# The weight conversions begin four steps earlier in a fused attention and expert kernel

## The chip, the core and the metric

The kernel runs on one core of a Trainium2 chip. The metric is the device time in microseconds, the median of three runs. The engines are named TensorE (PE in the rows, PEld its weight loads), VectorE (DVE), ScalarE (ACT), GpSimd (POOL) and SyncE (SP, whose queue issues all loads and stores here).

## The reference

Three layers follow one another: causal attention for 2 batches, 12 heads, 448 positions and 64 elements a head; a soft mixture of 8 experts with 4 slots each; and a gated product with three weight matrices, whose float64 elements the kernel reads as pairs of 32-bit words.

```python
scores = q @ k.T / sqrt(64); scores = where(causal, scores, -1e9)
attn = exp(scores - max); attn /= attn.sum + 1e-9; x = attn @ v        # x: 896 x 768
logits = x @ phi
d = softmax of logits over the tokens;  slot_input = d.T @ x           # 8 experts x 4 slots
for e in range(8): slot_out[e] = relu(slot_input[e] @ w1[e]) @ w2[e]
c = softmax of logits over the slots;   x = c @ slot_out
out = ((x @ w_a) * (x @ w_b)) @ w_out                                   # weights are float64
```

## The kernel before

**Pairs and steps.** Attention runs over 12 pairs of heads (`it` 0 to 11), each in four steps (`g` 0 to 3); a 13th round, `it` 12, only finishes the last pair. All instructions are written out by hand in the order in which each engine runs them. In a step of pair `it` TensorE makes score blocks (line 249, tile `s`), VectorE their negated maxima (lines 255 and 259, `nm`), ScalarE the exponentials with their sums (line 269, `p`), VectorE the reciprocals (lines 279 and 280, `rc`), and GpSimd scales the tiles by them (line 283). In the four steps of the next pair, TensorE transposes these tiles (line 296, `t`) and ScalarE copies them out (line 299, `pT`). In step 0 of the pair after that, TensorE multiplies them with the values (line 328, `v`), and ScalarE copies the product (line 332, `xT`). The product of pair 10 has fill matmuls before and within it (line 307), whose results nothing reads.

**Conversions.** A float64 weight matrix is read as tiles of 768 KB, `raw` 0 to 35, each half of a matrix block. A conversion is made of two activations on ScalarE (lines 162 and 163; in round 12 two GpSimd instructions, lines 155 and 158, in their place) and of two instructions on VectorE (lines 193 and 196). The VectorE part of a tile is written one conversion later than its ScalarE part, but when no tile below 32 is left to begin, what is still open is finished at once:

```python
while len(fin) > (lag if conv and conv[0] < limit else 0):
```

At the end of every step one conversion is begun, if the step's number is above `CVOFF` and the table `CVN` says so (three steps of four):

```python
step += 1
if step > CVOFF:
    conv_step(CVN[step % len(CVN)], LAG, NT1, "pool" if (it, g) > LASTQ else "act")
```

**Loads.** All loads are issued by SyncE, in the order of a list: `raw` tiles go round the four slots `r0` to `r3`, with a few expert weights (`w`) between them; a slot is loaded again when what it held has been used. After the 32 `raw` tiles, the four slots take expert weights. The next expert weights go to the slots `q0` to `q3` and then to `t0` and `t1`. These lie where the attention stage had its tiles, so that their loads wait for the end of that stage. The experts' matmuls (line 632, `h`, and line 673, `so`) use a tile, and its slot is loaded again.

Of the kernel before, what the change touches and what calls it, by code (L numbers as in the profile page):

```python
# [41 lines left out]
    (("rect", 28, 4, 0, 28), ("tri", 6, 2), ("sq", 28, 4)),  # L42
    (("sq", 8, 16),),
)
CVOFF = 7
NWARM = 32
NW2 = 4
LAG = 1
# [40 lines left out]
def moe_kernel(ctx: ExitStack, tc: tile.TileContext, pk, vt, phi, w1, w2, wab, wo, rsel, out):  # L89
# [94 lines left out]
    def conv_step(n, lag=LAG, limit=36, low="act"):  # L184
        for _ in range(n):
            if conv and conv[0] < limit:
                i = conv.pop(0)
                dst = conv_dst(i)
                done.append(i)
                fin.append((i,) + widen(raw[i], dst, 0, 768, low))  # L190
            while len(fin) > (lag if conv and conv[0] < limit else 0):
                i, di, b, ph = fin.pop(0)
                nc.vector.scalar_tensor_tensor(  # L193
                    out=b, in0=ph, scalar=-0x80000000, in1=b, op0=ALU.bitwise_and, op1=ALU.bitwise_or
                )
                nc.vector.scalar_tensor_tensor(  # L196
                    out=di, in0=di, scalar=3, in1=b, op0=ALU.logical_shift_left, op1=ALU.bitwise_or
                )
                used("raw", i)
# [288 lines left out]
    with tc.manual_schedule():  # L488
# [15 lines left out]
        for it in range(13):  # L504
            if 1 <= it < 12:
                load_v(it)
            for g in range(4):
# [25 lines left out]
# [3 lines that stand above are left out]
# [744 lines left out]
```

## Time and profile before

| | |
|---|---|
| median of 3 runs | 373.93 us (373.75 to 374.7) |
| the profiled execution | 375.18 us, with a span of 373.2 us from its first to its last instruction |
| mean granted clock of TensorE | 0.981 of full speed |
| TensorE, ScalarE, VectorE, GpSimd busy | 336.1, 206.4, 228.1 and 86.4 us of the span |
| read from memory | 87.33 MB |

The busy times are sums over the whole span, in which the stages have different limits. The attention stage ends at about 140 us; the experts and the weight products follow, and the last loads land before 280 us. The rows further down are read by stage: a row of a timeline has its start in us from the span's start, its length, the engine, the line, the operation, what it writes and reads, and, in brackets, how long the engine stood idle before it and what ended that.

### The profile page before, as it was taken

The page shows a single profiled execution, that of the slowest core. Times are in us where ns is not written, and L with a number is a line of the kernel's source. Part 1 is how long each engine was busy: PE and PEld are TensorE (multiplying, and loading weights), DVE is VectorE, ACT ScalarE, POOL GpSimd, SP SyncE. Part 2 cuts the span into 40 slices and gives each one's busy share as a digit, 9 for nine tenths or more (in the row PEclk, how much of TensorE's full clock was granted, in tenths as well). Part 3 has the DMA queues.
Part 4 walks back from the last instruction along what each step waited for, and adds up shares of the span by engine and source line. Part 5 has one row for each costly group of instructions (what it writes and reads, how often), then busy time and mean ns, then how long its engine had stood idle before and what let it go on. Part 6 is the DMA issues. An engine that isn't in the chain of part 4 may idle for free.

```text
span 373.2 us, 7002 instructions
## 1 busy us (share of the span) xinstructions
PE 336.1 (90%) x2587; PEld 205.3 (55%) x2587; DVE 228.1 (61%) x669; ACT 206.4 (55%) x475; POOL 86.4 (23%) x120
## 2 busy tenths in 40 slices
PE   8898898989989998979969889999899889999996
PEld 5564444545544655433423337543565358889995
DVE  3679999899999973020015887606956659933121
ACT  2799999999999971113007444513646742423221
POOL 2436756553556560010000000000000110301110
PEclk9999999899999999999998989999999989999999
DMA  7668799899677789999999999797920000001222
GB/s 277 269 202 284 266 336 347 289 368 304 236 271 258 243 255 355 419 419 415 417 344 374 380 364 341 245 356 225 420 122 2 0 2 0 1 2 42 86 84 84
DMA packets 20225, 90.52 MB, mean 243 GB/s; under 512 B 2336, under 2 KB 5024, under 8 KB 20192
## 3 DMA queue, kind: packets, MB, share of 16 engines
q1 hardware_dynamic: 20192, 90.09, 65.5%
q8 instruction: 20, 0.33, 0.3%
q14 instruction: 13, 0.11, 0.1%
HBM read 87.33 MB, written 2.75 MB: 241 GB/s over the span
## 4 chain that ended last, share of the span: by engine, by line
PE 45%; ACT 24%; DVE 16%; DMA 10%; issue 3%; POOL 2%; ACTq 0%; POOLq 0%; DVEq 0%
PE M L872 8%; PE o L1153 7%; ACT p L269 7%; DMA w<-in_w_dram 6%; ACT raw L163 4%; PE h L632 4%; PE ab L758 4%; DMA raw<-in_wo_dram 4%; PE so L673 3%; PE s L249 3%; ACT wab L162 3%; ACT pT L299 3%; DVE pf L814 3%; DVE pt L813 2%; PE t L296 2%
## 5 line engine op out<-in xcount | busy, mean ns | idle before, releaser
L283 POOL TENSOR_SCALAR p<-p,rc 128x448 f32<-128x448 f32 (+6 forms) x84 | 70.3, 848 | 61.3 <-DVE rc L280 28.7
L249 PE MATMUL s<-qk 64*64 64x448 f32 (+6 forms) x336 | 48.5, 403 | 0.0
L1057 POOL TENSOR_TENSOR cc<-gt,cc 128x512 fp32r<-128x512 f32 (+1 forms) x6 | 7.1, 1176 | 160.9 <-ACT cc L1056 160.9
L269 ACT ACTIVATE p<-s,nm 128x448 f32<-128x448 f32 (+6 forms) x84 | 40.4, 500 | 6.7 <-DVE nm L259 6.6
L872 PE MATMUL M<-wt,P_t 128*128 128x384 f32 x168 | 35.5, 356 | 3.7 <-DVE P_t L845 1.3
L193 DVE SCALAR_TENSOR_TENSOR raw<-raw 128x768 int32<-128x768 int32 x36 | 34.7, 965 | 4.4 <-ACT raw L163 2.6
L255 DVE TENSOR_REDUCE nm<-s 128x1 f32<-128x448 f32 (+6 forms) x84 | 31.7, 412 | 8.9 <-PE s L249 8.9
L296 PE MATMUL t<-ident,p 128*128 128x128 f32 x192 | 33.6, 293 | 2.9 <-POOL p L283 2.2
L872 PEld LDWEIGHTS M<-wt,P_t 128*128 128x128 f32 x168 | 29.2, 193 | 12.7 <-ACT wt L866 4.8
L328 PE MATMUL v<-pT,v 128*64 128x448 f32 (+3 forms) x192 | 26.9, 396 | 9.9 <-ACT pT L299 9.7
L163 ACT ACTIVATE raw<-raw 128x768 int32<-128x768 uint32 x35 | 33.0, 942 | 0.0
L632 PE MATMUL h<-w,sT 128*32 128x512 f32 x192 | 30.6, 614 | 2.0 <-ACT hs L645 1.6
L299 ACT ACTIVATE pT<-t 128x512 f32<-128x512 f32 x48 | 29.5, 620 | 2.7 <-PE t L296 2.5
L866 ACT ACTIVATE wt<-wo 128x384 fp32r<-128x384 f32 x48 | 21.8, 516 | 13.9 <-PE M L872 13.5
L867 DVE TENSOR_TENSOR wt<-wo,wt 128x384 fp32r<-128x384 f32 x48 | 23.9, 553 | 9.0 <-ACT wt L866 8.9
L249 PEld LDWEIGHTS s<-qk 64*64 64x64 f32 x336 | 20.0, 136 | 17.1 <-issue 11.0
L296 PEld LDWEIGHTS t<-ident,p 128*128 128x128 f32 x192 | 20.8, 142 | 15.4 <-POOL p L283 5.1
L758 PE MATMUL ab<-wab,sT 128*32 128x384 f32 x288 | 28.7, 517 | 0.5 <-DVE sT L597 0.5
L673 PE MATMUL so<-w,hpad 128*32 128x384 f32 x256 | 24.8, 493 | 4.2 <-DMA w<-in_w_dram 3.9
L196 DVE SCALAR_TENSOR_TENSOR wab<-wab,raw 128x768 int32<-128x768 int32 x24 | 27.1, 1130 | 0.8
L328 PEld LDWEIGHTS v<-pT,v 128*64 128x64 f32 (+1 forms) x192 | 10.9, 134 | 24.6 <-ACT pT L299 16.3
L162 ACT ACTIVATE wab<-raw 128x768 f32<-128x768 f32 x24 | 23.2, 967 | 0.0
(154 smaller groups left out, 516.2 us busy)
## 6 DMA issues: line engine op xcount, KB each, us to landing
w<-in_w_dram SPq DMA_DIRECT2D x64, 768.0 KB, 9.2
raw<-in_wab_dram SPq DMA_DIRECT2D x24, 768.0 KB, 5.0
raw<-in_wo_dram SPq DMA_DIRECT2D x12, 768.0 KB, 4.5
qk<-in_pk_dram SPq DMA_DIRECT2D x12, 448.0 KB, 5.1
v<-in_pk_dram SPq DMA_DIRECT2D x12, 192.0 KB, 4.8
out_dram<-ost SPq DMA_DIRECT2D x6, 384.0 KB, 2.3
v<-in_vt_dram SPq DMA_DIRECT2D x12, 32.0 KB, 4.5
out_dram<-ost SPq DMA_DIRECT2D x2, 192.0 KB, 1.9
```

The costliest lines, as they stand in the source:

```text
L163: nc.scalar.activation(out=pr[:, :, 0], in_=lw, func=AF.Copy, scale=2.0 ** -29, bias=-0.49999)
L193: nc.vector.scalar_tensor_tensor(out=b, in0=ph, scalar=-0x80000000, in1=b, op0=ALU.bitwise_and, op1=ALU.bitwise_or)
L249: nc.tensor.matmul(sb[r, o:o + n], lhsT=qT[r, 64 * i:64 * i + 64], rhs=kT[r, 0:n], start=False, stop=True, skip_group_check=True,)
L269: nc.scalar.activation(out=d["p"][:, POFF[i]:POFF[i] + n], in_=sb[:, o:o + n], func=AF.Exp, bias=d["nm"][:, c:c + 1], scale=0.125, accum_o ...
L283: nc.gpsimd.tensor_scalar(out=p[:, POFF[i]:POFF[i] + n], in0=p[:, POFF[i]:POFF[i] + n], scalar1=rc[:, CIX[i]:CIX[i] + 1], scalar2=1.0, op0 ...
L296: nc.tensor.transpose(ps[:, j, :], d["p"][:, o:o + 128], ident)
L299: nc.scalar.activation(out=dst, in_=ps, func=AF.Copy)
L328: nc.tensor.matmul(ps[r, 128 * kt:S], lhsT=lhsT, rhs=rhs, start=(kt == 0), stop=(kt == 3), skip_group_check=True)
L632: nc.tensor.matmul(ps[32 * g:32 * g + 32, :], lhsT=sT[:, 0, c, :], rhs=wt[8 * e + i // 3][:, 512 * (i % 3):512 * (i % 3) + 512], start=(i ...
L673: nc.tensor.matmul(so[32 * g:32 * g + 32, 0:384], lhsT=t[:, c, :], rhs=wt[8 * e + 4 + i // 4][:, 384 * (i % 4):384 * (i % 4) + 384], start ...
L758: nc.tensor.matmul(abps[q][32 * g:32 * g + 32, 0:384], lhsT=sT[:, 1, c, :], rhs=w[:, c % 2, 384 * g:384 * g + 384], start=(c == 0), stop=( ...
L872: nc.tensor.matmul(mps[k][h][:, 0:384], lhsT=l[:, f, :], rhs=r, start=(n == 0 and i == 0), stop=(n == 11 and i == 2))
```

## The change

The constant `CVOFF` goes from 7 to 3. The step's number counts from 1 with step 0 of pair 0, so the first conversion is begun in step 3 of pair 0 and no longer in step 3 of pair 1, and all later ones keep their distance.

```diff
-CVOFF = 7
+CVOFF = 3
```

What that does to the order is seen in three places. On ScalarE, from the last exponential of pair 0 on (`p0`; `raw0` is the first tile to be converted, `pT0` the copies of pair 0's transposes), before:

```order
L269 ACTIVATE p0_129,sm0_194<-s0_3_243,nm0_193 128x256
L299 ACTIVATE pT0_273<-t0_1_274 128x512
L269 ACTIVATE p1_134,sm1_225<-s1_0_263,nm1_224 128x448
L269 ACTIVATE p1_134,sm1_225<-s1_0_263,nm1_224 128x64
L299 ACTIVATE pT0_273<-t0_3_299 128x512
```

and after:

```order
L269 ACTIVATE p0_129,sm0_194<-s0_3_243,nm0_193 128x256
L162 ACTIVATE wab0_108<-raw0_182 128x768
L163 ACTIVATE raw0_182<-raw0_182 128x768
L299 ACTIVATE pT0_275<-t0_1_276 128x512
L269 ACTIVATE p1_134,sm1_225<-s1_0_265,nm1_224 128x448
L269 ACTIVATE p1_134,sm1_225<-s1_0_265,nm1_224 128x64
L162 ACTIVATE wab0_108<-raw1_188 128x768
L163 ACTIVATE raw1_188<-raw1_188 128x768
L299 ACTIVATE pT0_275<-t0_3_309 128x512
```

Tile 0 stands ahead of pair 0's first copy and tile 1 ahead of the second; in the order before, tile 0 came behind pair 1's last exponential.

On VectorE, at the end of step 0 of pair 11 and the start of its step 1 (`nm11` from `s11_1` are the maxima of step 1, those from `s11_2` of step 2), before:

```order
L193 SCALAR_TENSOR_TENSOR raw27_1412<-raw27_1412 128x768
L196 SCALAR_TENSOR_TENSOR wo1_1513<-wo1_1513,raw27_1412 128x768
L255 TENSOR_REDUCE nm11_1478<-s11_1_1586 128x1 x2
L259 TENSOR_SCALAR nm11_1478<-nm11_1478 128x2
L279 TENSOR_SCALAR rc11_1480<-sm11_1479 128x2
L280 RECIPROCAL rc11_1480<-rc11_1480 128x2
```

and after:

```order
L193 SCALAR_TENSOR_TENSOR raw30_1431<-raw30_1431 128x768
L196 SCALAR_TENSOR_TENSOR wo3_1556<-wo3_1556,raw30_1431 128x768
L193 SCALAR_TENSOR_TENSOR raw31_1474<-raw31_1474 128x768
L196 SCALAR_TENSOR_TENSOR wo3_1556<-wo3_1556,raw31_1474 128x768
L255 TENSOR_REDUCE nm11_1498<-s11_1_1609 128x1 x2
L259 TENSOR_SCALAR nm11_1498<-nm11_1498 128x2
```

Two tiles are finished ahead of step 1's maxima where one was, and the second of them is the tile that ScalarE converts in the same step 0.

On SyncE, at the end of the attention stage, before:

```order
L224 DMA v11_1543<-in_vt_dram 64x128
L148 DMA raw31_1584<-in_wo_dram 128x1536
L461 DMA w8_1640<-in_w1_dram 128x1536
L461 DMA w9_1664<-in_w1_dram 128x1536
L461 DMA w10_1728<-in_w1_dram 128x1536
L461 DMA w11_1732<-in_w1_dram 128x1536
L461 DMA w4_1804<-in_w2_dram 128x1536
```

and after:

```order
L148 DMA raw31_1474<-in_wo_dram 128x1536
L461 DMA w8_1537<-in_w1_dram 128x1536
L461 DMA w9_1561<-in_w1_dram 128x1536
L223 DMA v11_1563<-in_pk_dram 128x384
L224 DMA v11_1563<-in_vt_dram 64x128
L461 DMA w10_1603<-in_w1_dram 128x1536
L461 DMA w11_1607<-in_w1_dram 128x1536
L461 DMA w4_1804<-in_w2_dram 128x1536
```

The last `raw` tile and the first two expert weights of the ring slots now stand ahead of the values of pair 11; `w4`, the first for the slots `q0` to `q3`, follows the ring's four in both.

## Rows read from the trace of the kernel before

**Rows 1.** Attention windows: length, busy PE, PEld, DVE, ACT, POOL (count), clock, DMA, GB/s.

```profile
15.00:20.00 5.00, 5.00 (x49) 3.26 (x45) 3.30 (x14) 4.26 (x17) 2.02 (x5) 1.00 0.24 57
120.00:130.00 10.00, 9.33 (x91) 5.95 (x92) 9.48 (x23) 10.00 (x26) 6.26 (x7) 1.00 0.76 256
```

**Rows 2.** Timeline of ScalarE, pairs 0 to 2.

```profile
13.95 0.60 ACT L299 ACTIVATE pT<-t 128x512 f32<-128x512 f32 x1 [1.62 <-PE t L296]
15.83 0.60 ACT L299 ACTIVATE pT<-t 128x512 f32<-128x512 f32 x1 [0.37 <-PE t L296]
17.71 0.60 ACT L299 ACTIVATE pT<-t 128x512 f32<-128x512 f32 x1 [0.37 <-PE t L296]
20.07 0.93 ACT L162 ACTIVATE wab<-raw 128x768 f32<-128x768 f32 x1
20.88 0.94 ACT L163 ACTIVATE raw<-raw 128x768 int32<-128x768 uint32 x1
22.23 0.55 ACT L332 ACTIVATE xT<-v 128x448 f32<-128x448 f32 x1 [0.41 <-PE v L328]
23.37 0.63 ACT L269 ACTIVATE p<-s,nm 128x448 f32<-128x448 f32 x1
```

**Rows 3.** DMA issues, 3.8 to 4.2 us: count, size, us to landing.

```profile
raw<-in_wab_dram SPq DMA_DIRECT2D x1, 768.0 KB, 8.7
```

**Rows 4.** Timeline of GpSimd, pairs 1 and 10.

```profile
19.85 0.94 POOL L283 TENSOR_SCALAR p<-p,rc 128x320 f32<-128x320 f32 x2 [0.39 <-ACT pT L299]
119.67 2.42 POOL L283 TENSOR_SCALAR p<-p,rc 128x320 f32<-128x320 f32 x2 [0.73 <-ACT raw L163]
```

**Rows 5.** Timeline of ScalarE, pair 11.

```profile
124.77 0.93 ACT L163 ACTIVATE raw<-raw 128x768 int32<-128x768 uint32 x1
126.03 0.62 ACT L269 ACTIVATE p<-s,nm 128x384 f32<-128x384 f32 x1
127.40 0.66 ACT L299 ACTIVATE pT<-t 128x512 f32<-128x512 f32 x1
```

**Rows 6.** Timeline of VectorE, pairs 2 and 11.

```profile
22.91 0.96 DVE L196 SCALAR_TENSOR_TENSOR wab<-wab,raw 128x768 int32<-128x768 int32 x1
124.86 0.74 DVE L255 TENSOR_REDUCE nm<-s 128x1 f32<-128x384 f32 x2
```

**Rows 7.** Timeline of TensorE, pair 5 and pair 11.

```profile
64.03 1.35 PE L328 MATMUL v<-pT,v 128*64 128x320 f32 x12 [1.68 <-ACT pT L299]
126.76 0.66 PE L296 MATMUL t<-ident,p 128*128 128x128 f32 x4
127.25 0.51 PE L307 MATMUL v<-ident 128*128 128x64 bf16 x12
128.12 0.97 PE L328 MATMUL v<-pT,v 128*64 128x448 f32 x4 [0.35 <-ACT pT L299]
131.11 1.34 PE L328 MATMUL v<-pT,v 128*64 128x320 f32 x12 [0.57 <-ACT pT L299]
132.39 1.42 PE L296 MATMUL t<-ident,p 128*128 128x128 f32 x8
134.12 1.14 PE L296 MATMUL t<-ident,p 128*128 128x128 f32 x8
```

**Rows 8.** Windows with the clock at half, columns as in rows 1.

```profile
65.30:68.70 3.40, 3.40 (x20) 1.92 (x17) 3.30 (x8) 3.32 (x8) 1.69 (x2) 0.50 0.93 285
195.00:198.40 3.40, 2.95 (x20) 1.15 (x22) 2.75 (x4) 1.79 (x2) 0.00 (x0) 0.50 1.00 288
```

**Rows 9.** Timeline of SyncE's queue, end of the attention stage.

```profile
146.61 0.33 SPq L461 DMA_DIRECT2D w<-in_w_dram  x1
```

**Rows 10.** DMA issues, first 134.9 to 136 us, then 146.5 to 146.7.

```profile
w<-in_w_dram SPq DMA_DIRECT2D x1, 768.0 KB, 4.3
w<-in_w_dram SPq DMA_DIRECT2D x1, 768.0 KB, 8.4
```

**Rows 11.** Waits of TensorE, 181 to 195 us: total, times, longest.

```profile
PE so L673 <- DMA w<-in_w_dram: 2.9, 5, 1.1
```

## The prediction, made before the changed kernel ran

> **What bounds the kernel now.** I read the stages first. In the attention stage ScalarE is the engine without idle time: 10.00 of 10 us from 120 on, against 4.26 of 5 from 15 on [rows 1]. So the stage runs at ScalarE's pace, and a conversion costs it two activations whose starts lie 0.81 us apart, 1.6 us in all [rows 2]. After the attention stage the weights arrive in one unbroken stream of 768 KB loads. The load issued at 135.28 landed after 4.3 us; the one at 146.61 needed 8.4, because others were ahead of it [rows 9, 10]. From the waits of TensorE between 183 and 194 us one sees who sets the end there: five waits for that stream, 2.9 us together [rows 11]. Behind them, 3.40 us run at half the granted clock, the lower of the two levels (1.2 of 2.4 GHz) [rows 8].
>
> So two things can move the end by d, by which the first expert matmul starts later than now: TensorE's own work, which has 2.9 us of waits to give back, and the stream.
>
> **The change part by part.** *What moves.* Conversions run in three of every four steps. The first moves four steps ahead, so three more are queued on ScalarE ahead of pair 2 (raw 0 to 3, where only raw 0 was); the last, raw 31, goes from GpSimd in the closing steps to ScalarE in step 0 of pair 11. Pairs 2 to 10 have three each as before; pair 11 has one in place of three.
>
> *The start.* Three more conversions are 4.8 us of ScalarE. Is there room? The gaps ahead of its copies and of pair 0's product are 1.62, 0.37, 0.37 and 0.41 us [rows 2]. An instruction starts about 0.1 us before the one ahead of it ends (20.07 + 0.93 against 20.88), so each gap holds 0.1 more work. Raw 0 needs 1.6 and has 1.7: it fits in whole, ahead of the copy of 13.95. Raw 1 was issued at 3.80 and landed 8.7 us later, at 12.5, in time [rows 3]; it makes the copy of 15.83 late by 1.6 - 0.48 = 1.12 us, and the next gap brings that to 0.64. Raw 2 adds 1.6: 2.2 late. Raw 3 then takes the place that raw 0 had at 20.07, and the last gap takes 0.5. Pair 2's first exponential goes from 23.37 to about 25.1. The gaps swallow 3.1 of the 4.8 us; the lag is **1.7**. Its lower bound is 1.5 (ScalarE never waits after raw 3), its upper 4.8 (nothing fits). I take 1.7 because every gap has its row. Raw 3 and raw 4 are loaded earlier too, where the transfers ran at 57 GB/s between 15 and 20 us [rows 1], so they delay no other load. VectorE's two instructions for each of these conversions lie beside that ScalarE time.
>
> One row speaks against this. GpSimd scales two tiles in 0.94 us alone, and in 2.42 beside VectorE's two instructions of a conversion [rows 4]; in pair 1 it now gets such neighbours, and I have let the transposes wait for that (0.2 of the 1.7). The Trainium skill states why: GPSIMD Engine Reference, section Specifications, says that GpSimd shares its SBUF interfaces with VectorE and that instructions with two SBUF inputs contend. By that rule the lag is 1.7, with the scaling at its speed alone 1.5; the trace agrees with the rule.
>
> *The middle.* ScalarE stays full and the order in a pair is the same: the lag is carried, not paid back.
>
> *Pair 11.* Here two conversions less, 3.2 us of ScalarE, should give it back. The order of VectorE says otherwise. The lag of one conversion between ScalarE and VectorE falls away for the last one, so raw 30 and raw 31 are both finished ahead of the maximum of step 1, and raw 31's part waits for ScalarE's second activation. That one ended at 124.77 + 0.93 = 125.70 for the conversion now in this place [rows 5]; with the lag, 127.4. Two VectorE instructions of 0.96 (the row without a neighbour on GpSimd) end at 129.4, the two maxima take 0.74 [rows 6], the small scaling behind them a little: the exponentials of step 1 start at about 130.4 in place of 126.03, **4.4 late** [rows 5]. Queued behind raw 31 on VectorE are all of that pair's maxima and reciprocals; ScalarE waits for the maxima, GpSimd for the reciprocals. The copy of 127.40 follows at 131.8, and with it the product matmuls of 128.12 at 132.5. The fill matmuls behind them take as long as now, so the rest of the product goes from 131.11 to 134.9, 3.8 late; the wait on GpSimd in the transposes behind it (eight took 1.42 us at 132.39 and 1.14 at 134.12, so about 0.3) goes, as GpSimd has no conversions beside it any more. d is **3.5 us** [rows 7]. Bounds: 0.8 (ScalarE alone decides: 1.7 less the 0.57 that TensorE waited and that 0.3) and 6.6 (a lag of 4.8).
>
> *The clock in pair 11.* TensorE has finished the transposes and the small fills ahead of 132.5 at about 129.5 (the fills of 127.25 end at 127.76 now, 1.7 later then) and then stands for 3.0 us. The clock's fall at 65.3 followed a gap of 1.68 us [rows 7, 8]. I take it that it falls here: half the clock over 3.4 us takes at most 1.7 us, and I put 1.5 (as at 195, where TensorE was busy for 2.95 of 3.40 and lost half of it). It costs nothing elsewhere, since the product matmuls are on the path. So d is **5.0**.
>
> *The stream.* The loads into the four ring slots, which now stand ahead of the others when the stage ends, come earlier by three conversions and are in before the attention buffers open; the load of 146.61 then finds a queue that is nearly empty and lands 4.3 us after its issue, as the one of 135.28 did, and not 8.4 [rows 9, 10]. But its issue hangs on the end of the attention stage, d later. The stream is d - 4.1 against now: **+0.9**.
>
> *TensorE's path.* d - 2.9 for the waits that it gives back, less c for the clock behind them. With no waits between 183 and 194 I expect no half clock at 195; c is half of 2.95, 1.5 [rows 8]. The path is 5.0 - 2.9 - 1.5 = +0.6. The later of the two counts: **+0.9 us**. Behind 200 us both are needed (loads for the experts and for raw 34), and the order there is unchanged.
>
> The profiled execution took 375.18 us (373.2 of span), so 376.1 for it; the median of the three runs is 1.25 lower, 373.93, which makes **374.8**.
>
> **The rivals.** *No fall of the clock in the last pair*: d is 3.5, the stream -0.6, the path -0.9: -0.6, 373.3. For it: the wait of 0.57 us at 131.11 and that of 0.35 at 128.12 brought none; against it, this gap is nearly twice the one ahead of 65.3 [rows 7].
>
> *The half clock at 195 stays* (the slower one): c is 0, the path is 5.0 - 2.9 = +2.1, 376.0. It decides from c below 1.0 on. For it: TensorE still waits for VectorE's copies there; against it, the five waits ahead are gone. With d at 3.5 it gives +0.6, 374.5.
>
> On both the Trainium skill has a rule, in TensorE: Matmul & The Clock Gate, part The HAM clock gate: the throttled state is the default and activity releases it. By that the fall in pair 11 and its absence at 195 are both likelier, 374.8; the rows at 65.3 and 195 agree, as TensorE stood ahead of both.
>
> *The last pair does pay back*: VectorE's double part is hidden, d is 0.8, the stream -3.3, the path -3.6: 370.6. For it: 3.2 us of ScalarE really go; against it: maxima queue behind raw 31.
>
> *The start fills less*: a lag of 2.7 in place of 1.7 makes d 6.0 and the stream +1.9, 375.8.
>
> That the change does nothing is excluded by the order.
>
> **How the numbers follow.** Forecast 0.33, no fall 0.24, half clock stays 0.16 (with d 3.5: 0.08), paid back 0.13, less filled 0.06. A change of 0.3%, 1.1 us, is about what a measurement here can tell from none. Faster: paid back and the tail of no fall, 0.15. Slower: half clock stays, less filled, and about 0.09 of the forecast's own spread (0.3 us above its value is enough), 0.31. Same: 0.54. The range leaves out the paid-back case below and the tail of the two slowest above: 372.5 to 376.2.
>
> **What would show it.** Raw 0's activations at 12.2; pair 2's first exponential at 25.1; a gap of 2.7 us on ScalarE and of 3.0 on TensorE in pair 11; the first expert matmul 5.0 us later than now; no waits for weights from 183 on; full clock there. Wrong it is if pair 11's step 1 starts within 2 us of ScalarE's being free, or if the clock falls in other places than these.

## The result, and the profile after

The changed kernel took **375.06 us** (median of 20 runs, 373.45 to 378.48), the kernel before, run beside it, 373.48 (20 runs, 371.65 to 376.64). The ratio is **1.006, 95% interval 1.0036 to 1.0084**: 1.3 to 3.1 us longer. In a second comparison it was 1.0037 (1.0008 to 1.0067). So the change costs about 1.8 us, more than the forecast's 0.9, in the forecast's direction. That 375.06 lies so near the forecast 374.8 is in part luck: the three runs from which the forecast started have a median of 373.93, 0.45 above that of the 20.

The two profiled executions hide that: their spans are 372.9 us after and 373.2 before, the mean clock 0.981 in both. The half clock lies in other places, though: before at 65, 195, 219 and 297 us, after at 34, 79, 113 and 133. Such stretches shift the stages against each other, so the stages are compared one by one. Ahead of the first three of those after, TensorE stood for 1.66 or 1.67 us before a product; the first of these gaps is the one in brackets here:

```profile
32.94 1.34 PE L328 MATMUL v<-pT,v 128*64 128x320 f32 x12 [1.66 <-ACT pT L299]
```

**The start.** ScalarE's timeline of the changed kernel, pairs 0 to 2 (answers to [rows 2]; start, length, engine, line, operation, tiles, idle time before it):

```profile
8.32 0.63 ACT L269 ACTIVATE p<-s,nm 128x448 f32<-128x448 f32 x1 [6.09 <-DVE nm L259]
...
12.06 0.91 ACT L162 ACTIVATE wab<-raw 128x768 f32<-128x768 f32 x1
13.78 0.60 ACT L299 ACTIVATE pT<-t 128x512 f32<-128x512 f32 x1
...
15.17 0.93 ACT L162 ACTIVATE wab<-raw 128x768 f32<-128x768 f32 x1
16.80 0.57 ACT L299 ACTIVATE pT<-t 128x512 f32<-128x512 f32 x1
...
22.09 0.98 ACT L162 ACTIVATE wab<-raw 128x768 f32<-128x768 f32 x1
23.72 0.59 ACT L332 ACTIVATE xT<-v 128x448 f32<-128x448 f32 x1
24.94 0.63 ACT L269 ACTIVATE p<-s,nm 128x448 f32<-128x448 f32 x1
```

From 12.06 on, no row of ScalarE has idle time in brackets any more. From pair 0's first exponential to pair 2's it takes 24.94 - 8.32 = 16.62 us. Before, pair 0 began at 8.47:

```profile
8.47 0.63 ACT L269 ACTIVATE p<-s,nm 128x448 f32<-128x448 f32 x1 [6.25 <-DVE nm L259]
...
123.06 0.65 ACT L269 ACTIVATE p<-s,nm 128x448 f32<-128x448 f32 x1
...
148.38 2.78 PE L632 MATMUL h<-w,sT 128*32 128x512 f32 x24
```

and pair 2 at 23.37 [rows 2], 14.90 us. The lag is 1.72. The second and third row are the start of pair 11 and the first expert matmul, 25.32 us apart.

**Pair 11.** VectorE after (answers to [rows 6]):

```profile
125.41 0.96 DVE L193 SCALAR_TENSOR_TENSOR raw<-raw 128x768 int32<-128x768 int32 x1
126.40 1.12 DVE L196 SCALAR_TENSOR_TENSOR wo<-wo,raw 128x768 int32<-128x768 int32 x1
128.29 0.96 DVE L193 SCALAR_TENSOR_TENSOR raw<-raw 128x768 int32<-128x768 int32 x1 [0.77 <-ACT raw L163]
129.28 0.96 DVE L196 SCALAR_TENSOR_TENSOR wo<-wo,raw 128x768 int32<-128x768 int32 x1
130.16 0.75 DVE L255 TENSOR_REDUCE nm<-s 128x1 f32<-128x384 f32 x2
```

ScalarE (answers to [rows 5]), and under it TensorE (answers to [rows 7]):

```profile
125.64 0.63 ACT L269 ACTIVATE p<-s,nm 128x448 f32<-128x448 f32 x1
...
127.35 0.91 ACT L163 ACTIVATE raw<-raw 128x768 int32<-128x768 uint32 x1
128.14 0.58 ACT L299 ACTIVATE pT<-t 128x512 f32<-128x512 f32 x1
131.20 0.58 ACT L269 ACTIVATE p<-s,nm 128x384 f32<-128x384 f32 x1 [2.47 <-DVE rc L279]
...
132.59 0.60 ACT L299 ACTIVATE pT<-t 128x512 f32<-128x512 f32 x1
```

```profile
129.83 0.51 PE L307 MATMUL v<-ident 128*128 128x64 bf16 x12
133.25 1.76 PE L328 MATMUL v<-pT,v 128*64 128x448 f32 x4 [2.91 <-ACT pT L299]
134.94 2.30 PE L307 MATMUL idle_x<-ident 128*128 128x128 bf16 x24
...
154.12 1.06 PE L632 MATMUL h<-w,sT 128*32 128x512 f32 x8
```

One reads the chain upwards: the product waits 2.91 us for a copy of ScalarE, which stands behind exponentials that waited 2.47 for the maxima on VectorE (the row names line 279, the instruction just behind the maxima), which stood behind tile 31's two instructions (128.29, 129.28), which waited 0.77 for ScalarE's second activation of that tile. The four product matmuls then take 1.76 us where 0.97 stood [rows 7], and the fills 2.30 where they took 1.51 (the row of before comes first), because the clock is at half there (answers to [rows 8]; length, busy time of PE, PEld, DVE, ACT and POOL with counts, granted clock, DMA share, GB/s):

```profile
129.02 1.51 PE L307 MATMUL idle_x<-ident 128*128 128x128 bf16 x24
```

```profile
133.22:136.63 3.41, 3.38 (x21) 1.99 (x22) 0.67 (x5) 1.83 (x7) 2.02 (x5) 0.50 0.75 296
195.00:198.40 3.40, 2.18 (x23) 1.17 (x19) 0.56 (x1) 0.00 (x0) 0.00 (x0) 1.00 1.02 242
```

From 125.64 to the first expert matmul at 154.12 it takes 28.48 us, 3.16 more than before.

**The loads.** SyncE's queue after (answers to [rows 9]) and the times from issue to landing of the same four loads in the same order (answers to [rows 10]): the first into `t0`, the third of that group, raw 32 and raw 34.

```profile
152.34 0.33 SPq L461 DMA_DIRECT2D w<-in_w_dram  x1
155.23 0.33 SPq L461 DMA_DIRECT2D w<-in_w_dram  x1
163.88 0.33 SPq L148 DMA_DIRECT2D raw<-in_wo_dram  x1
192.78 0.33 SPq L148 DMA_DIRECT2D raw<-in_wo_dram  x1
```

```profile
w<-in_w_dram SPq DMA_DIRECT2D x1, 768.0 KB, 4.3
w<-in_w_dram SPq DMA_DIRECT2D x1, 768.0 KB, 6.4
raw<-in_wo_dram SPq DMA_DIRECT2D x1, 768.0 KB, 12.7
raw<-in_wo_dram SPq DMA_DIRECT2D x1, 768.0 KB, 11.6
```

They landed at 156.6, 161.6, 176.6 and 204.4. Before, the first landed at 146.61 + 8.4 = 155.0 [rows 9, 10]; the other three, issued at 149.49, 158.66 and 188.02, took

```profile
w<-in_w_dram SPq DMA_DIRECT2D x1, 768.0 KB, 9.1
raw<-in_wo_dram SPq DMA_DIRECT2D x1, 768.0 KB, 15.0
raw<-in_wo_dram SPq DMA_DIRECT2D x1, 768.0 KB, 13.7
```

and landed at 158.6, 173.7 and 201.7. So the stream is 1.6 us late at `t0`, 3.0 at the third load, 2.9 at raw 32 and 2.7 at raw 34, with a first expert matmul that is 154.12 - 148.38 = 5.74 us late. TensorE's waits for weights after, from 148 to 200 us and then from 200 to 240 (answers to [rows 11]; before they were 2.9 us, and 0.3 in the later stretch):

```profile
PE so L673 <- DMA w<-in_w_dram: 0.5, 1, 0.5
PE h L632 <- DMA w<-in_w_dram: 2.1, 2, 1.2
```

Of the waits of 2.9 us 0.5 are left, and 1.8 us come back behind 200.

### The profile page after: what moved, and what is told of

The parts are those of the page before. It is cut to its first block, busy times and chain, and to the rows that moved or that the text cites. A ratio compares the mean times of both kernels' runs of the same rounds, so it can differ in the third digit from the quotient of the medians.

```text
span 372.9 us, 7003 instructions
## 1 busy us (share of the span) xinstructions
PE 335.1 (90%) x2587; PEld 206.0 (55%) x2587; DVE 227.2 (61%) x669; ACT 207.8 (56%) x477; POOL 83.3 (22%) x118
## 4 chain that ended last, share of the span: by engine, by line
PE 45%; ACT 23%; DVE 22%; POOL 4%; DMA 3%; issue 3%; ACTq 0%; POOLq 0%; DVEq 0%
PE o L1153 7%; PE M L872 7%; ACT p L269 6%; PE so L673 4%; PE h L632 4%; ACT raw L163 4%; DVE pf L814 4%; POOL p L283 4%; PE ab L758 4%; DMA raw<-in_wo_dram 3%; DVE pt L813 3%; PE s L249 3%; ACT pT L299 3%; ACT wab L162 3%; PE t L296 2%
## 5 line engine op out<-in xcount | busy, mean ns | idle before, releaser
L249 PE MATMUL s<-qk 64*64 64x448 f32 (+6 forms) x336 | 50.1, 413 | 0.2 <-DMA qk<-in_pk_dram 0.2
L328 PE MATMUL v<-pT,v 128*64 128x448 f32 (+3 forms) x192 | 27.7, 404 | 12.1 <-ACT pT L299 11.9
L296 PE MATMUL t<-ident,p 128*128 128x128 f32 x192 | 34.5, 300 | 2.8 <-POOL p L283 2.4
L872 PEld LDWEIGHTS M<-wt,P_t 128*128 128x128 f32 x168 | 28.4, 188 | 12.6 <-ACT wt L866 4.0
L632 PE MATMUL h<-w,sT 128*32 128x512 f32 x192 | 29.1, 600 | 3.0 <-DMA w<-in_w_dram 2.1
L758 PE MATMUL ab<-wab,sT 128*32 128x384 f32 x288 | 26.8, 488 | 0.5 <-DVE sT L597 0.5
```

The costliest lines, as they stand in the source:

```text
L249: nc.tensor.matmul(sb[r, o:o + n], lhsT=qT[r, 64 * i:64 * i + 64], rhs=kT[r, 0:n], start=False, stop=True, skip_group_check=True,)
L296: nc.tensor.transpose(ps[:, j, :], d["p"][:, o:o + 128], ident)
L328: nc.tensor.matmul(ps[r, 128 * kt:S], lhsT=lhsT, rhs=rhs, start=(kt == 0), stop=(kt == 3), skip_group_check=True)
L632: nc.tensor.matmul(ps[32 * g:32 * g + 32, :], lhsT=sT[:, 0, c, :], rhs=wt[8 * e + i // 3][:, 512 * (i % 3):512 * (i % 3) + 512], start=(i ...
L758: nc.tensor.matmul(abps[q][32 * g:32 * g + 32, 0:384], lhsT=sT[:, 1, c, :], rhs=w[:, c % 2, 384 * g:384 * g + 384], start=(c == 0), stop=( ...
L872: nc.tensor.matmul(mps[k][h][:, 0:384], lhsT=l[:, f, :], rhs=r, start=(n == 0 and i == 0), stop=(n == 11 and i == 2))
```

## The experiments

Theory: the double finish of tiles 30 and 31 on VectorE stalls the last pair, the clock falls behind that stall, and what this costs beyond the cover of the load queue is the loss. Rivals: the crowded start or the moved loads cost it; the falls of the clock late in the run do. Every trace is cut in the way shown above: the **start's lag** is the time from pair 0's first exponential to pair 2's, less 14.90; the **last pair** is the time from pair 11's first exponential to the first expert matmul, less 25.32.

| kernel | start's lag | last pair | ratio to before (95%) |
|---|---|---|---|
| changed kernel | 1.72 | +3.16 | 1.006 (1.0036 to 1.0084) |
| e0, the same again | 1.73 | +3.18 | 1.0037 (1.0008 to 1.0067) |
| e1, lag kept | 1.68 | -1.01 | 0.9947 (0.9918 to 0.9976) |
| e12, lag kept, again | 1.74 | -1.00 | 0.9936 (0.9908 to 0.9964) |
| e8, lag kept, CVOFF 4 | 1.68 | -0.35 | 0.9953 (0.9925 to 0.9981) |
| e2, tile 31 in round 12 | 2.95 | -1.39 | 0.9988 (0.9959 to 1.0018) |
| e3, double finish in before | 2.09 | +3.12 | 1.0037 (1.0007 to 1.0066) |
| e4, 80 fills | 1.70 | +1.58 | 1.0057 (1.003 to 1.0084) |
| e7, 110 fills | 1.70 | +1.59 | 1.0027 (0.9996 to 1.0057) |
| e6, start alone | 1.71 | 0.00 | 0.9956 (0.9927 to 0.9984) |
| e9, lag kept, delayed | 1.71 | +0.82 | 1.0027 (0.9997 to 1.0057) |
| e10, before, delayed | 0.00 | +1.81 | 1.0031 (0.9992 to 1.007) |
| e11, before, delayed more | 0.00 | +4.47 | 1.0045 (1.0016 to 1.0074) |

> The changed kernel itself, on the same chip as the next three, so that they can be held against it. Theory: 1.003 to 1.009 of before, about 374.3 us where before has 372.2; the first expert matmul at 153.5 to 154.5, half clock behind the TensorE gap at 133.

e0 confirms the cut: both parts agree with the first execution to 0.02 us. The profiled executions of e2 and e3 had a stretch of half clock at 12 us, which the lag of those two rows contains.

**The lag kept (e1, and again e12).**

```diff
-            while len(fin) > (lag if conv and conv[0] < limit else 0):
+            hold = lag if (conv and conv[0] < limit) or (low == "act" and limit == NT1 and n) else 0
+            while len(fin) > hold:
```

> As the changed kernel, but the VectorE part of tile 31 keeps its lag of one conversion: it is written at the end of step 1 of pair 11 and no longer ahead of that step's maxima. Theory (the double finish of tiles 30 and 31 stalls the last pair and opens the TensorE gap behind which the clock falls): step 1's exponentials start at 128.3 to 129.0 in place of 131.20, no TensorE gap above 1.5 us ahead of pair 10's product and no half clock there, the first expert matmul at 149.2 (148.5 to 150.5; 148.38 before, 154.12 in the changed kernel), the time 371.5 us (370.5 to 372.5), 0.99 to 1.00 of before. Rival (the crowded start or the moved loads are what costs): the first expert matmul may come earlier, but the time stays at 374.5 or above, 1.003 or more.

> The first experiment's kernel once more, on the chip of the three delayed ones: 0.995 of before (0.992 to 0.998) and the first expert matmul 1.0 us earlier, counted from the last pair's first exponential, than in the kernel before.

In the kernel that ran, tile 31's VectorE part came later than I wrote, in round 12, since a step without a conversion finishes nothing. ScalarE, VectorE and TensorE of e1 in pair 11:

```profile
123.85 0.63 ACT L270 ACTIVATE p<-s,nm 128x448 f32<-128x448 f32 x1
...
126.35 0.59 ACT L300 ACTIVATE pT<-t 128x512 f32<-128x512 f32 x1
126.82 0.58 ACT L270 ACTIVATE p<-s,nm 128x384 f32<-128x384 f32 x1
```

```profile
125.65 0.74 DVE L256 TENSOR_REDUCE nm<-s 128x1 f32<-128x384 f32 x2
...
130.97 1.06 DVE L194 SCALAR_TENSOR_TENSOR raw<-raw 128x768 int32<-128x768 int32 x1
```

```profile
128.87 0.97 PE L329 MATMUL v<-pT,v 128*64 128x448 f32 x4 [0.32 <-ACT pT L300]
...
148.16 2.78 PE L633 MATMUL h<-w,sT 128*32 128x512 f32 x24
```

The exponentials of step 1 no longer wait, the gap ahead of the product is 0.32 us, the product takes 0.97. The crowded start and the early loads are still there (lag 1.68), and the kernel is faster than before: 0.9947, in the repetition 0.9936. That puts the whole loss on the last pair; the rivals of the start and of the loads fall. The first expert matmul, at 148.16, comes a little earlier than the 148.5 to 150.5 that I expected. The third rival has little for it either: both profiled executions of the changed kernel ran at full clock from 138 to 372 us, and the mean granted clock of all of e0's runs, 0.983, is nearly that of the kernel before on the same chip, 0.984. e1 is the fastest version that was run.

**Tile 31 back in round 12 (e2).**

```diff
+                    if it == 11:
+                        conv_step(0, 0, NT1)
+                    else:
                         conv_step(CVN[step % len(CVN)], LAG, NT1, "pool" if (it, g) > LASTQ else "act")
```

> As the changed kernel, but tile 31 is held back for round 12 and done on GpSimd there, so that pair 11 has no conversion on ScalarE at all and the end of the stage has its old order. Theory: the first expert matmul at 148.5 (147.5 to 149.5), as 4.8 us of ScalarE are gone from pair 11 against a lag of 1.7, TensorE then being the limit; the time 372 us (371 to 373). Rival (start or loads): 374.5 or above. Rival (tile 31 on ScalarE in place of GpSimd is what costs): also no slower than before, but then the run with the lag kept is still slower.

The time is 0.9988 of before, no difference that can be told from none. The last pair is 1.39 us shorter, as expected, but tiles 30 and 31 are both finished only in round 12 here, so the last two ring slots are loaded later (137.25 us for the last, in e1 133.26), and the head start of the loads is partly undone. That the move of tile 31 off GpSimd costs anything is refuted by e1, where it is on ScalarE.

**The double finish alone (e3).** In the kernel before:

```diff
-                    conv_step(CVN[step % len(CVN)], LAG, NT1, ...)
+                    conv_step(CVN[step % len(CVN)], 0 if (it, g) == (11, 0) else LAG, NT1, ...)
```

> As the kernel before, but tiles 27 and 28 are both finished on VectorE ahead of step 1's maxima in pair 11: the double finish alone, without an earlier start. Theory: step 1's exponentials go from 126.03 to about 129.0, a TensorE gap of some 2.5 us ahead of pair 10's product, the first expert matmul 2 to 3 us later (150.4 to 151.4), 1.5 more where the clock falls behind the gap. The time moves by less than 1 us (373.0 to 374.5), because up to 4.1 us of delay at the end of the stage is covered by the queue of loads that already stands there, and 2.9 us by waits of TensorE. Rival (the double finish is hidden): the first expert matmul within 0.7 us of 148.38.

ScalarE and TensorE of e3 in pair 11:

```profile
129.03 0.58 ACT L269 ACTIVATE p<-s,nm 128x384 f32<-128x384 f32 x1 [2.47 <-DVE rc L279]
```

```profile
131.08 1.76 PE L328 MATMUL v<-pT,v 128*64 128x448 f32 x4 [2.91 <-ACT pT L299]
```

The two waits are those of the changed kernel to the hundredth, and the clock falls behind them. The kernel is 1.0037 of before: 1.4 us longer (0.3 to 2.5), where I expected less than 1 us.

**The gap filled (e4, e7).**

```diff
-KEEPV = {10: 12, 11: 6}
+KEEPV = {10: 80, 11: 6}      # e7: 110
```

> As the changed kernel, with 80 in place of 12 fill matmuls (128x64) ahead of pair 10's product, 68 x 0.043 = 2.9 us of them, so that TensorE is busy in the gap. Theory: the clock stays full from 133 to 137, the product matmuls take 0.97 us again and the fills within it 1.5, the first expert matmul at 152.6 (154.12 in the changed kernel), the time 1.0 to 1.5 us below the changed kernel: 373.6 to 374.1. Rival (the clock's fall is not tied to the gap, or costs nothing): half clock there as before, or the first expert matmul within 0.4 us of 154.1.

> As the changed kernel with 110 in place of 12 fill matmuls ahead of pair 10's product (80 took 2.50 us and left a gap of 0.91 us), so that the gap is closed and only the delay by the double finish is left. Theory (a fall of the clock there is paid in full): full clock from 132 to 137, the first expert matmul 1.5 us earlier than in the changed kernel on the same chip, the time 1.2 to 1.6 us below it. Rival (the time lost to the clock is not won back, because falls in other places come instead): the same median as the changed kernel, with a mean granted clock that is no higher.

TensorE of e7, and the window around it (columns as above):

```profile
128.40 3.37 PE L307 MATMUL v<-ident 128*128 128x64 bf16 x110
131.84 0.97 PE L328 MATMUL v<-pT,v 128*64 128x448 f32 x4
```

```profile
128.00:137.00 9.00, 8.94 (x167) 7.28 (x168) 4.55 (x18) 5.17 (x16) 3.26 (x7) 1.00 0.68 251
```

In both kernels the clock stays full and the last pair is 3.16 - 1.59 = 1.57 us shorter: that is the price of the fall, and what remains, 1.59, is the stall. The 1.0 to 1.6 us that I expected to win are not seen in the time: e7 is 1.0027 of before where the changed kernel on its chip is 1.0037, 0.4 us and less than the uncertainty of either; e4 is 1.0057. Their profiled executions have half clock at 173 and 217 instead, where the changed kernel's had none, and the mean granted clock of their twelve runs each, 0.979 in e4 and 0.981 in e7, is no higher than e0's 0.983. That is what e7's rival says: falls in other places come instead. e4's own runs show what such falls cost: the four at 0.986 took 371.99 to 373.09 us, the eight at 0.973 to 0.977 374.47 to 375.63. So the fall is shown to hang on the gap; that avoiding it wins time is not shown.

**The start alone (e6).** Pair 5 does no conversion, and from pair 6 on all stands as before:

```diff
-                    conv_step(CVN[step % len(CVN)], LAG, NT1, "pool" if (it, g) > LASTQ else "act")
+                    conv_step(CVN[step % len(CVN)] if it != 5 else 0, LAG, NT1, "pool" if (it, g) > LASTQ else "act")
```

> As the changed kernel, but the three conversions of pair 5 are left out of the table, so that from pair 6 on everything stands where the kernel before has it: the earlier start alone. Theory (the start costs 1.7 us of lag and nothing else): the lag is there at pair 2 and gone behind pair 5, the last pair has no gap above 1 us, the first expert matmul at 148.4 (147.9 to 149.1), the time within 0.4% of before. Rival (the crowded start or the earlier loads cost the time): the first expert matmul at 150 or later, 1.004 or more.

Pair 5 of e6 on ScalarE, its first exponential and the next pair's:

```profile
56.56 0.69 ACT L269 ACTIVATE p<-s,nm 128x448 f32<-128x448 f32 x1
64.06 0.54 ACT L332 ACTIVATE xT<-v 128x448 f32<-128x448 f32 x1 [1.86 <-PE v L328]
65.19 0.63 ACT L269 ACTIVATE p<-s,nm 128x448 f32<-128x448 f32 x1
```

The pair takes 8.63 us where its neighbours take 10.85 to 10.88: three conversions, 4.8 us of ScalarE, gave back 2.2, because ScalarE then waits for TensorE (1.86). With 1.71 lost at the start that is a net gain of 0.5; the ratio, 0.9956, says 0.6 to 2.7 us. Part of that is the clock of these runs, 0.99 in the mean against 0.984 before. Both the ratio and the first expert matmul (146.31, expected from 147.9 on) lie outside what I expected, on the early side. An earlier start costs nothing that a pair without conversions does not pay back.

**One conversion less in front (e8).** e1 with `CVOFF = 4`:

> The lag kept for the last tile, as in the first experiment, with CVOFF 4 in place of 3: the start is two conversions earlier than before in place of three, and tile 31 is begun in step 2 of pair 11, so that pair 11 has two conversions on ScalarE. Theory (with the double finish gone, each conversion moved out of the last pair gives 1.6 us of ScalarE there as long as that is the limit, less the lag of the start): the first expert matmul at 148.5 to 149.5 (148.16 with three), the time within 0.3% of the first experiment, 0.993 to 0.998 of before. Rival (the gain of the first experiment came from elsewhere): 1.00 or more.

The time is as expected, 0.9953. The first expert matmul, at 150.75, is later than expected; that execution had half clock at 34, 79 and 113 us, and its last pair is 0.66 us longer than e1's, as one more conversion stands in it. The lag of the start is the same 1.68 with two conversions as with three, so the third was free there.

**Delay behind the stage (e9, e10, e11).** More fill matmuls just ahead of the second batch's softmax, in e1 (e9) and in the kernel before (e10, e11):

```diff
-KEEPB = (6, 20, 5, 14, 6, 8)
+KEEPB = (46, 20, 5, 14, 6, 8)      # e11: 94
```

> The first experiment's kernel with 40 more fill matmuls (0.053 us each) behind the attention stage: the first expert matmul is 1.9 us later and nothing else is changed. Theory (in that kernel the queue of weight loads is empty when the stage ends, so each us of delay is a us of the whole): the time rises by the whole 1.9 us, from 0.995 to about 1.000 of before. Rival (loads still cover the delay): within 0.3% of the first experiment's kernel on the same chip.

> The kernel before with the same 40 fill matmuls behind the attention stage. Theory (its queue holds loads for 2.7 us more when the stage ends, and TensorE waits 2.9 us for them later): the first expert matmul 1.9 us later, raw 34 and the time unchanged, 0.998 to 1.002 of before. Rival (a delay there is paid in full): 1.005.

> The kernel before with 88 fill matmuls more at that place, 4.5 us of delay, close to the 4.9 us that the changed kernel has from its start and its last pair. Theory (what counts of it is what goes beyond 2.7 us: the queue runs empty at the load into t0 and again at the third load behind the stage): 1.8 us longer than before, 1.005 (1.003 to 1.008). With my forecast's 4.1 us in place of 2.7 it would be 0.4 us, 1.001; paid in full it would be 1.012.

These ask what a delay d of the first expert matmul costs where the start and the last pair are untouched. e11, with 4.47 us, is 1.0045: 0.6 to 2.8 us. Paid in full it would be 1.012; by the forecast's rule 1.001; by d - 2.7, 1.005. Only the last lies within the interval, 1.0016 to 1.0074. e10 with 1.81 us is 1.0031, an interval that holds both its theory and the rival. e9 is 0.0091 above e12 on the same chip, 3.4 us with an uncertainty of about 1.5, for 1.82 us of delay: it is paid, as expected where the queue is empty, and the excess stays unexplained.

## Why the prediction was right or wrong

**The start: right.** Lag 1.7 forecast, 1.72 measured; raw 0 fits into the first gap (12.06), and pair 2 begins at 24.94 (25.1 forecast). GpSimd's scaling of the two tiles of [rows 4] in pair 1 stretched from 0.94 to 2.21 us. The Trainium skill (GPSIMD Engine Reference, section Specifications) says that GpSimd shares its SBUF interfaces with VectorE, with contention when a VectorE instruction has two SBUF inputs; the trace agrees. On ScalarE it cost next to nothing: no row there has idle time from 12.06 on, so the 0.2 us that the forecast set aside for this isn't seen as a wait.

**The middle: the lag is carried, but more half clock came on top.** From pair 2 to pair 11 it took 100.70 us after and 99.69 before, where the lag was to be carried unchanged; e1, which has no half clock before 214 us, took 99.19. The difference is half clock at 34, 79 and 113 us, against one such stretch before. It makes the 5.74 us at the first expert matmul larger than the part of the start and the last pair, 1.72 + 3.16 = **4.9 us, against the forecast d of 5.0**. By the forecast's own words, falls in other places than those it named are a sign of being wrong, and these it did not see coming. Whether the edit has a share in them stays open: e0 and e8 had all three and e4 and e9 two of them, but e1, e2, e7 and e12, in the same order of instructions up to pair 11, had none of them, nor had any kernel with the old start.

**Pair 11: right.** Waits of 2.47 us on ScalarE and 2.91 on TensorE (2.7 and 3.0 forecast), from tile 31's VectorE part, and the clock at half behind them. The stall is worth 1.59 us (1.8 by the forecast's terms, 3.5 less 1.7) and the fall 1.57 (1.5). In three profiled executions with the gap (the changed kernel twice, e3) the clock fell there, in two with fills in it (e4, e7) it did not. The Trainium skill's rule (TensorE: Matmul & The Clock Gate, part The HAM clock gate), that the throttled state is the default and activity releases it, agrees with that.

**TensorE's path: too hopeful.** Of the 2.9 us of waits that it was to give back, 0.5 remained ahead of 200 us and 1.8 came back behind it. And c, the 1.5 us of half clock at 195, is a weak term: that the changed kernel runs at full clock there came true in both its profiled executions, but of the two executions of one and the same kernel e12 had half clock at 192.6 and e1 had none there. What one execution shows there is not the kernel's own. (The rival in which the half clock stays decides from c below 1.2 on, as 2.1 - c is then above 0.9, and not from 1.0 as written.)

**The stream: the term that was mis-sized.** The forecast was d - 4.1 = +0.9, from the one load into `t0` (8.4 us before, 4.3 with an empty queue). That load did as forecast: 5.74 - 4.1 = 1.6 us late. But the stream lost another 1.4 us by the third load of that group (landed at 161.6 against 158.6), and kept nearly all of it to raw 34. So the cover was not 4.1 us but about 5.74 - 3.0 = 2.7, and the change's own 4.9 us become **+2.2 in place of +0.9**. Of the measured ratios one says 2.2 and one 1.4 us; e1 at 1.68 - 1.01 - 2.7 = -2.0 (measured -2.0 and -2.4), e8 at -1.4 (-1.8) and e11 at +1.8 (+1.7) follow the same rule. The 2.7 is read from one pair of traces; e11 is the run that tested it at a value named beforehand. e4 and e7 should be at +0.6 and were at +2.1 and +1.0; falls of the clock in other places, as seen above, go with that. e3 should be at +0.4 and was at +1.4. There the double finish also holds back the second load into the ring slots (issued at 135.57, before at 132.77), and the third load behind the stage lands 2.3 us late (160.9 against 158.6) for a first expert matmul that is 3.5 late: the cover is 1.2 and not 2.7. e9 should be at -0.2 and was at +1.0, and that stays open. Why the stream loses those 1.4 us once its queue has been nearly empty isn't shown; no run varied it alone.

The rival "the last pair does pay back" came true only with the lag kept: the same three conversions moved are then a gain, because the last pair loses 1.0 us in place of gaining 3.2.

## What to carry to other kernels

When work is moved earlier by a constant, look at what the code does at its last item: here a rule that finishes the queue at once put two VectorE instructions of the last tile ahead of the critical maxima, and that, not the move, cost the time. A delay in front of a stream of loads is covered only as far as the queue is still full, and the cover has to be read at several loads, not at the first. A term read from one stretch of half clock in one execution is a term of that execution.

## What the runs showed of the hardware that was not expected

Executions of the same kernel on one chip differ by up to 5.5 us (the kernel before beside e9 to e12: 370.56 to 376.04 in 34 runs), and that goes with the clock: the seven of these runs with a mean granted clock of 0.994 or 0.995 took 370.56 to 371.56 us, the six at 0.972 to 0.976 373.09 to 376.04. The stretches of half clock lie in different places: two profiled executions of the kernel with the lag kept had them at 214.7 alone, and at 66.3 and 192.6. Here are the first of these, in the weights, and one of e4 in the attention stage (the last column but two is the granted clock); TensorE was busy nearly throughout while the clock was at half:

```profile
214.70:218.00 3.30, 3.30 (x11) 1.34 (x10) 3.30 (x19) 0.94 (x2) 0.00 (x0) 0.50 1.00 414
```

```profile
112.00:115.20 3.20, 3.20 (x16) 1.69 (x16) 3.10 (x9) 3.15 (x8) 1.46 (x2) 0.50 1.02 406
```

Ahead of the falls in the middle of the attention stage TensorE always did the same. The fourteen traces have 62 gaps of 1.65 to 1.73 us ahead of a product between 20 and 120 us, and all 18 stretches of half clock that begin there follow one of them; behind the other 44 the clock stayed full. Behind the gap of 2.9 us in pair 11 it fell three times of three. So the one row at 65.3 from which the forecast started shows that a gap of 1.7 us can be followed by a fall, and not that it is.

The loss of 1.4 us in the stream of loads behind a queue that had run nearly empty was not expected either. Eleven of the fourteen traces have such a hole among the ten loads from the one into `t0` on, where a landing comes 3.0 to 3.6 us after the one before it in place of 1.9. The three without it (before, e6 and e10) still had loads for 4.3 us or more queued when that one was issued. Its cause stays open.
